# Value rows of 68 numbers per head instead of 66, and the block table's scratch inside another tile

## The chip, the cores and the metric

The kernel runs on one core of a Trainium2 chip. The time is device time in microseconds (us): 266.18 us is the median of 5 runs before the change, which lie between 265.45 and 267.64 us. Lower is better.

## The reference

Two layers follow each other. The first is a sparse attention over 4 batches of 8 heads, 768 positions and 64 numbers per head. Positions are cut into 24 blocks of 32. A query block sees its own block and its two neighbours, the first and last block, and three blocks that a table (`sampled_blocks`) draws for it. The first and last query blocks see everything.

```
scores = scale * q @ k.T ; masked entries -> -1e9
attn   = exp(scores - max) / (sum + 1e-9)
x      = attn @ v                       # 4 x 8 x 768 x 64 -> 3072 x 512
h      = x @ w_in ; r = max(h, 0) ; out = (r * r) @ w_out   # 512 -> 2048 -> 512
```

## The kernel before, in words

The order of all instructions is written out ahead of time. A planner in the kernel (`run_schedule`) holds a list of tasks with an estimated cost, a due key and the engines that may take it, and emits them one by one; after that each engine runs its own fixed list and only waits for semaphores. The estimates are constants in the file, so a change of a tile's width does not enter them.

**Batches 0 and 1 (dense with a mask).** For each pair of heads, TensorE multiplies keys by queries into PSUM (L500, and L504 for the mask rows of the first query columns), ScalarE takes the exponential into the tile `pT` (L511), VectorE multiplies by the 0/1 mask `MK` (L518), and TensorE multiplies `pT` by the values (L540). The value tile `VN` (two buffers, L370) holds, in each of 128 partitions, 6 chunks of positions x 8 heads x `VS` bf16 numbers. `VS` is 66 (L57): 64 numbers of the value, then ones. A matmul of L540 reads the first 65 (`VW`) of a head's row, so that its 65th output column is the sum of the weights, and L548 and L550 divide by it. Its output `po` is a PSUM tile whose heads stand 65 numbers apart; the pitch there is `VW`, not `VS`. The loop of L540 alternates the two heads of a pair: first head, second head, first head, and so on. Since a row has 66 numbers of 2 bytes, the first head of pair a starts 264a bytes into its chunk and the second 132 bytes after it.

**Batches 2 and 3 (sparse).** Values are cast into the same `VN` (L283 out of `cast_v`), written whole to a copy in DRAM, `vd` (L635), which has 800 rows of 8 heads x `VS` numbers, 1056 bytes; 32 rows of zeros are added to it (L631). For each of 12 query tiles, keys are gathered by VectorE and ScalarE into `KG`, and values are brought back from `vd` into a tile `VG`: the window rows and the rows of the global blocks by SP's queue (L693, L699), the rows of the drawn blocks by indirect DMAs that GpSimd (POOL) issues (L703, one for each query block, 96 rows each, by the row numbers `idx`). There are two `VG`: one lies in the raw-input tile `RAW`, the other in the mask tile `MK`; DMA rows name these. Scores are L715 and L720, exponentials L727, and values L761: four query blocks at a time in the four column groups of TensorE, weights of 128 x 32, moving rows of 65 numbers out of `VG` or `VN`, outputs again 65 apart.

**The second layer** runs between these tasks as TensorE becomes free: L810 (512 -> 2048), L819 or L821 (relu), L830 or L832 (square), L860 (2048 -> 512), then a copy and a store.

**The block table.** At the start VectorE builds the 24 x 24 table of visible blocks in a scratch tile `al` (24 x 4 x 24 fp32, L380, written by L386 to L391, reduced by L393), which sets the mask rows `bm` (L394). `KG1` (L331) is a tile of 4096 bf16 per partition that later holds one of the two `KG`; at the start its first 2304 numbers hold three helper tables, and the numbers from 2304 on serve later as scratch for the row numbers (L585, six pieces of 72 fp32).

Of the kernel before, what the change touches and what calls it, by code (L numbers as in the profile page):

```python
# [12 lines left out]
F32 = mybir.dt.float32  # L13
# [12 lines left out]
def kernel(  # L26
# [12 lines left out]
    B, H, S, D = q.shape  # L39
    block = 32  # L40
    nb = S // block
    n_rand = sampled_blocks.shape[1]
# [11 lines left out]
    TWM = 768  # L54
    NU = B * HP
    VW = D + 1
    VS = D + 2  # L57
    ND = 2
    NT = NCH
    SEQ = [NT - 1] + list(range(NT - 1))  # L60
# [5 lines left out]
    consts = ctx.enter_context(tc.tile_pool(name="consts", bufs=1))  # L66
# [264 lines left out]
    KG1 = consts.tile([P, HP * 4 * 256], BF, name="KG1")  # L331
# [36 lines left out]
    for i in range(2):  # L368
        QKB.append(consts.tile([P, HP, 2, S], BF, name=f"QK{i}"))
        VN.append(consts.tile([P, NCH, H, VS], BF, name=f"VN{i}"))  # L370
        G.memset(VN[i][:, :, :, D:VS], 1.0)
    QK = [QKB[u // HP % 2][:, u % HP] for u in range(NU)]
# [4 lines left out]
    V.tensor_copy(out=oh.rearrange("a (n p) -> a n p", p=P), in_=place.rearrange("a (p n) -> a n p", n=NCH))  # L377
    edge = consts.tile([nb, 2], F32, name="edge")
    pm = consts.tile([nb, 2, nb], F32, name="pm")
    al = consts.tile([nb, n_rand + 1, nb], F32, name="al")  # L380
    V.tensor_scalar(out=pm[:, 0, :], in0=rel, scalar1=-1.0, scalar2=None, op0=AOP.is_ge)
    V.tensor_scalar(out=edge[:, 0:1], in0=row, scalar1=0.0, scalar2=None, op0=AOP.is_equal)
    V.tensor_scalar(out=edge[:, 1:2], in0=row, scalar1=float(nb - 1), scalar2=None, op0=AOP.is_equal)
# [27 lines left out]
    KG = [x.rearrange("p (a i c) -> p a i c", a=HP, i=4) for x in KG]  # L411
    VG = [flat[1][:, 0:8 * H * VS], MK.rearrange("p n s -> p (n s)")[:, 0:8 * H * VS]]
    VG = [x.rearrange("p (i c d) -> p i c d", i=4, c=2) for x in VG]
# [163 lines left out]
    at16 = consts.tile([1, (nb - 2) * n_rand], I32, name="at16")  # L577
    vd = {b: dram.tile([S + block, H * VS], BF, name=f"vd{b}") for b in range(ND, B)}
    picked_of = sbb.rearrange("p (q r two) -> p q r two", r=n_rand, two=2)[:, 1:nb - 1, :, 0]
# [44 lines left out]
    def zero_rows(part, e):  # L624
        if part == 0:
            z = work.tile([P, 2, 512], BF, name="pT", tag="pT", bufs=PT_BUFS).rearrange("p h c -> p (h c)")
            V.memset(z[0:block, 0:H * VS], 0.0)
            stmp["z"] = z[0:block, 0:H * VS]
        else:
# [582 lines left out]
```

## Time and profile before

| what | value |
|---|---|
| median of 5 runs | 266.18 us (265.45 to 267.64) |
| the profiled execution's own time | 265.65 us |
| its span, first to last instruction | 263.9 us |
| granted TensorE clock | 1.00 |
| busy: VectorE / ScalarE / POOL | 155.4 / 199.2 / 138.2 us |
| DMA moved | 46.40 MB in 62992 packets, 176 GB/s on average |
| value rows back from `vd` by SP's queue | 12 + 8 transfers of 198 KB, 4 of 99 KB, 16 of 66 KB |
| value rows back by POOL's indirect DMAs | 44 (20 into `RAW`, 24 into `MK`), 916 to 1173 ns of POOL each |
| `vd` written | 2 transfers of 792 KB |

A row of the chain of work reads: start in the span, length, engine, tile and line, and how many instructions. PE is TensorE, DVE is VectorE, ACT is ScalarE, SP and POOL issue DMAs. A group row reads: instruction, count, shortest, median and longest duration in ns, first and last start. Durations of matmuls are from issue to a modelled end and overlap; what a matmul costs TensorE is the distance from one start to the next, or a run's length in the chain divided by its count.

### The profile page before, as it was taken

The numbers are of one execution on the slowest core, as the hardware profiler recorded it, in microseconds if no ns is written. First come the engines' busy times: TensorE is split into PE (matmuls) and PEld (weight loads), VectorE is DVE, ScalarE is ACT, GpSimd is POOL, SyncE is SP. The second block draws the span as 40 slices with busy tenths as digits, with TensorE's granted clock in tenths as the row PEclk, the third lists the DMA queues.
The fourth block names the chain that finished last, engine by engine and source line by source line (L and its number), as shares of the span: only waits on it lengthen the run. The fifth ranks groups of instructions, "written<-read, shape, count | busy, mean of one in ns | idle before, by whom it ended". The sixth has DMA issues, their size and how long they took to land.

```text
span 263.9 us, 8712 instructions
## 1 busy us (share of the span) xinstructions
PE 254.5 (96%) x3552; PEld 163.0 (62%) x3552; DVE 155.4 (59%) x452; ACT 199.2 (75%) x303; POOL 138.2 (52%) x175
## 2 busy tenths in 40 slices
PE   8999999999998899999999999999999999999994
PEld 5768866577565456656566566545665566655554
DVE  7797789999999997874554622145165535121000
ACT  3898979898989898889868898422986578945920
POOL 4391625505479700668978685540767577802610
PEclk9999999999999999999999999999999999999999
DMA  6999999979936965089966998968616645231012
GB/s 195 367 269 207 202 224 318 363 158 240 182 93 151 203 153 166 36 220 299 227 162 132 266 181 220 277 202 209 137 28 161 185 127 135 73 102 42 0 40 82
DMA packets 62992, 46.40 MB, mean 176 GB/s; under 512 B 22088, under 2 KB 57832, under 8 KB 62952
## 3 DMA queue, kind: packets, MB, share of 16 engines
q1 hardware_dynamic: 56072, 36.79, 54.8%
q0 software_dynamic: 6336, 8.66, 16.7%
q8 instruction: 28, 0.46, 0.7%
q10 hardware_dynamic: 544, 0.39, 0.5%
q14 instruction: 12, 0.10, 0.2%
HBM read 37.32 MB, written 7.98 MB: 172 GB/s over the span
## 4 chain that ended last, share of the span: by engine, by line
PE 68%; DVE 18%; DMA 5%; issue 3%; ACT 2%; SPq 2%; POOL 1%; DVEq 0%; ACTq 0%; POOLq 0%
PE py L860 25%; PE X L810 21%; DVE pT L518 10%; PE po L540 4%; PE X L761 4%; PE X L715 4%; PE X L500 3%; DMA RAW<-in_k_dram 2%; PE F L810 2%; ACT pT L511 2%; DMA MK<-vd,idx 2%; DVE xq L550 2%; PE X L860 2%; DVE qc L283 1%; SPq L300 1%
## 5 line engine op out<-in xcount | busy, mean ns | idle before, releaser
L832 POOL TENSOR_TENSOR g<-r 128x384 bf16<-128x384 f32 (+1 forms) x55 | 51.2, 936 | 80.4 <-ACT r L819 63.4
L860 PE MATMUL py<-w_out_sb,g 128*128 128x512 bf16 (+2 forms) x384 | 91.9, 368 | 0.2 <-DVE ys L283 0.2
L810 PE MATMUL X<-xT,w_in_sb 128*128 128x384 bf16 (+1 forms) x512 | 84.0, 313 | 0.0
L511 ACT ACTIVATE pT<-X 128x1024 bf16<-128x1024 f32 (+1 forms) x76 | 70.7, 979 | 9.9 <-PE X L500 6.6
L810 PEld LDWEIGHTS <-w_in_sb 128*128 128x128 bf16 x640 | 55.6, 98 | 28.0 <-issue 1.9
L819 ACT ACTIVATE r<-X 128x768 f32<-128x768 f32 (+1 forms) x61 | 46.2, 761 | 14.5 <-PE X L810 12.2
L860 PEld LDWEIGHTS <-g 128*128 128x128 bf16 x416 | 35.9, 98 | 29.5 <-issue 2.0
L518 DVE TENSOR_TENSOR pT<-pT,MK 128x1024 bf16<-128x1024 bf16 x60 | 50.3, 866 | 2.3 <-ACT pT L511 2.1
L830 ACT ACTIVATE g<-r 128x384 bf16<-128x384 f32 (+1 forms) x65 | 33.6, 540 | 1.3
L769 DVE RECIPROCAL rss<-X 128x8 f32<-128x8 f32 x12 | 2.5, 208 | 51.4 <-PE X L761 48.4
L727 ACT ACTIVATE pT<-X 128x1024 bf16<-128x1024 f32 x28 | 27.2, 1028 | 7.3 <-PE X L715 7.3
L540 PEld LDWEIGHTS <-pT 128*128 128x128 bf16 x576 | 22.5, 97 | 8.5 <-issue 4.2
L540 PE MATMUL po<-VN,pT 128*128 128x65 bf16 x576 | 24.8, 193 | 2.3 <-DVE xT L283 1.5
L703 POOL DMA_INDIRECT MK<-vd,idx x24 | 22.7, 945 | 6.8 <-issue 5.8
L500 PE MATMUL X<-QK 64*128 64x256 bf16 (+1 forms) x336 | 25.4, 257 | 0.0
L281 ACT COPY ys<-py 128x512 f32<-128x512 f32 (+1 forms) x17 | 9.9, 581 | 17.9 <-PE py L860 17.9
L703 POOL DMA_INDIRECT RAW<-vd,idx x20 | 19.1, 953 | 5.8 <-issue 4.6
L283 POOL CAST VN<-RAW 128x768 bf16<-128x768 f32 x15 | 14.8, 988 | 11.8 <-DMA RAW<-in_v_dram 11.6
L500 PEld LDWEIGHTS <-QK 64*128 64x128 bf16 x336 | 13.6, 94 | 9.9 <-issue 6.3
L283 DVE CAST qc<-RAW 128x768 bf16<-128x768 f32 (+3 forms) x22 | 14.0, 656 | 2.4 <-DMA RAW<-in_q_dram 1.3
L283 POOL CAST qc<-RAW 128x768 bf16<-128x768 f32 (+1 forms) x13 | 13.4, 1041 | 1.6 <-DMA RAW<-in_q_dram 0.8
L761 PEld LDWEIGHTS <-pT 128*32 128x32 bf16 x896 | 9.2, 95 | 5.6 <-issue 5.5
(109 smaller groups left out, 255.7 us busy)
## 6 DMA issues: line engine op xcount, KB each, us to landing
RAW<-in_v_dram SPq DMA_DIRECT2D x16, 384.0 KB, 7.4
RAW<-in_k_dram SPq DMA_DIRECT2D x15, 384.0 KB, 5.6
out_dram<-ys SPq DMA_DIRECT2D x21, 256.0 KB, 3.1
RAW<-in_q_dram SPq DMA_DIRECT2D x12, 384.0 KB, 4.0
MK<-vd SPq DMA_DIRECT2D x12, 198.0 KB, 3.8
w_in_sb<-in_moe_w_in_dram POOLq DMA_DIRECT2D x4, 512.0 KB
w_out_sb<-in_moe_w_out_dram POOLq DMA_DIRECT2D x4, 512.0 KB, 16.7
vd<-VN SPq DMA_DIRECT2D x2, 792.0 KB
```

The lines of the kernel that those rows point to most:

```text
L283: (V if e == "DVE" else G).tensor_copy(out=out, in_=in_)
L500: nc.tensor.matmul(ps[:, h, j * w:(j + 1) * w], QK[i][hs, 1, ksl], QK[i][hs, 0, qsl], start=j == 0, stop=not add, skip_group_check=True)
L511: A.activation(out=pT[:, :, 0:n], in_=stile.pop(a)[:, :, 0:n], func=AF.Exp, scale=scale)
L518: V.tensor_tensor(out=pT, in0=pT, in1=m[:, None].broadcast_to([P, 2, len(cs), w]), op=AOP.mult)
L540: nc.tensor.matmul(po[:, qc, h, :], pT[:, h, j * w + qc * P:j * w + (qc + 1) * P], VT[i][:, n, h, 0:VW], start=(n == 0 and qc == 0 and h = ...
L703: G.indirect_dma_start(out=VG[x][0:96, i, 1, :], out_offset=None, in_=vd[b][:, :], in_offset=bass.IndirectOffsetOnAxis(ap=idx[:, n:n + 1], ...
L727: A.activation(out=pT, in_=stile.pop((b, t, s_)), func=AF.Exp, scale=scale)
L810: nc.tensor.matmul(htile[T, f][:, i], w_in_sb[:, kc, (f + i) * P:(f + i + 1) * P], xT[b][:, kc, c0:c0 + w], start=(kc == 0), stop=(kc == K ...
L819: A.activation(out=to, in_=src, func=AF.Relu)
L830: A.activation(out=g, in_=r, func=AF.Square)
L832: (G if e == "POOL" else V).tensor_mul(out=g, in0=r, in1=r)
L860: nc.tensor.matmul(ytile[T, i], gtile[T, f][:, ts * P:(ts + 1) * P], w_out_sb[:, f, cs[0]:cs[1]], start=(f == 0), stop=(f == NF - 1))
```

## The change

The row of a head becomes 68 numbers (136 bytes): in `VN`, in the copies `vd` (rows of 1088 bytes), in the zero rows and in both `VG`. 4 ones follow each value instead of 2. Matmuls still read 65 numbers of a row, and PSUM keeps its pitch of 65. The two `VN` take 192 bytes more per partition each, 384 together, and `al`, which took 384 bytes, is no longer a tile of its own: it lies in the last 192 bf16 of `KG1`, behind the helper tables and behind the later scratch.

```diff
-    VS = D + 2
+    VS = D + 4
...
-    al = consts.tile([nb, n_rand + 1, nb], F32, name="al")
+    al = KG1[0:nb, KG1.shape[1] - 2 * (n_rand + 1) * nb:].bitcast(F32).rearrange("q (r j) -> q r j", j=nb)
```

On each engine the changed program has the same instructions in the same order and waits for the same engines; what differs is the extent of the ones' memsets (L371: 128 x 96 numbers before, 128 x 192 after), of the zero rows (L627, L631), of every DMA that writes or reads `vd` (rows of 528 numbers before, 544 after), and the addresses inside `VN`, `VG` and `vd`.

## The prediction

> **What bounds the kernel now.** I read first the page's busy row and chain of work, to see which engine ends last.
>
> ```profile
> PE 254.5 (96%) x3552; PEld 163.0 (62%) x3552; DVE 155.4 (59%) x452; ACT 199.2 (75%) x303; POOL 138.2 (52%) x175
> ...
> PE 68%; DVE 18%; DMA 5%; issue 3%; ACT 2%; SPq 2%; POOL 1%; DVEq 0%; ACTq 0%; POOLq 0%
> ```
>
> TensorE (PE) is busy 96% of the span, and 68% of the chain is its own work. Next the table of busy time by stretch (start:end, length, then busy us and count for PE, weight loads, VectorE, ScalarE, POOL; clock, DMA share, GB/s), to see whether that holds in the stages that read value rows.
>
> ```profile
> 20.00:60.00 40.00, 39.16 (x610) 28.67 (x607) 35.34 (x82) 35.35 (x49) 14.39 (x18) 1.00 1.06 242
> 60.00:95.00 35.00, 32.71 (x395) 21.50 (x392) 33.58 (x59) 31.44 (x42) 21.62 (x19) 1.00 0.81 174
> 95.00:110.00 15.00, 14.92 (x207) 9.57 (x202) 11.96 (x27) 13.19 (x18) 2.21 (x3) 1.00 0.39 115
> ...
> 130.00:180.00 50.00, 49.94 (x832) 29.66 (x831) 18.82 (x76) 34.08 (x58) 32.24 (x38) 1.00 0.90 207
> 180.00:240.00 60.00, 59.74 (x923) 35.98 (x922) 25.07 (x118) 41.19 (x67) 33.80 (x44) 1.00 0.47 120
> ```
>
> From 95 us on PE leaves almost nothing free; from 20 to 95 us it shares the path with VectorE's mask multiplications. So a ns saved or added on a matmul with value rows counts almost in full late and in part early. Third, the chain in order of time, for what one such matmul costs (start, length, what).
>
> ```profile
> 98.74 0.74 PE po L540 x24
> ...
> 139.51 0.93 PE X L715 x32
> ...
> 148.07 0.62 PE X L761 x63
> ...
> 213.30 0.92 POOL MK L703
> 214.22 0.30 issue
> 214.53 4.53 DMA MK<-vd,idx
> 219.05 0.04 issue
> 219.10 0.64 PE X L761 x56
> ```
>
> L540 costs 0.74/24 = 30.8 ns for 65 columns, L715 0.93/32 = 29.1 ns for 64, with the same 128 x 128 weight loads. The last lines show the one place where value rows from DRAM set the path: a gather lands 4.53 us after its issue and the matmuls of L761 wait for it.
>
> **The value matmuls of the dense half, L540.** Inside its runs the starts do not stand 30.8 ns apart but alternate: the 288 steps from a first head to its second have a median of 29 ns, the 246 from a second head to the next first one a median of 33. L715, with a new weight load for each matmul too, goes on at 29. So the second head of a pair costs 4 ns more. Two things set it apart: its moving row starts 132 bytes after the first head's, 4 past a multiple of 8, where first heads start at 264a bytes (0 or 8 past a multiple of 16); and its output starts 65 x 4 = 260 bytes after, also 4 past a multiple of 8. The change mends the first alone: heads start at 136h bytes, again 0 or 8 past a multiple of 16, where the first heads already run at 29 ns. If the moving row is the cause, 288 x 4 ns = 1.15 us of PE time go. How much lies on the path: the least is the chain's share of L540, 4% of 263.9 = 10.3 us of 576 x 31 ns = 17.9 us, 58%, so 0.66 us; the most is all of it, 1.15 us, if PE's order passes every ns on. I take the middle, -0.9 us. If the output is the cause, it is 0. A loss here I exclude: no head comes to an offset at which one runs today at over 29 ns.
>
> The Trainium skill bears on both. "PSUM — Partial Sum Buffer", section "Specifications (TRN2)", gives PSUM lines of 8 bytes and says that output patterns that aren't contiguous slow matmuls: that speaks against this change, as the second head's output still starts inside such a line, and by it the 4 ns would stay. "TensorE: Matmul & The Clock Gate", section "Back-to-back issue gap", gives N/2.4 + 2.5 ns, an estimate of 29.6 ns for 65 columns: by it L540 has 1.4 ns too much on average and 0.8 us in all to win. No row of before decides between the two.
>
> **The value matmuls of the sparse half, L761.** 0.62 us for 64, four column groups at once: 16 groups at some 30 ns after a start of two slower ones. In the tiles with no wait inside, at most three steps per tile are 4 to 6 ns over the 29 of the rest. At most 12 x 3 x 5 ns = 0.18 us can go, at least 0; they don't alternate with the heads as in L540. I take -0.05.
>
> **More bytes from and to `vd`.** SP's returns are 20 x 198 + 4 x 99 + 16 x 66 = 5412 KB, the gathers 44 x 96 x 1056 bytes = 4.46 MB, the writes 2 x 792 KB: some 11.6 of 46.4 MB, and 2/66 = 3.0% of them, 0.35 MB, is added. The packets' own time in the trace is 386 us (1056 bytes), 73 (2112 bytes) and 287 (gathers), 746 us over 16 engines: 46.6 us, of which 3% is 1.4 us. That is the upper end, if each transfer were waited for. The nearest row, the waits of PE from 132 to 240 us, has one such wait, 0.3 us:
>
> ```profile
> PE X L761 <- DMA MK<-vd,idx: 0.3, 1, 0.3
> ```
>
> There 3% of 4.53 us is 0.14 us. The other tiles hide it: for instance the gathers issued at 168.0 to 171.7 us serve matmuls at 179.1. Two are tight: those issued up to 143.0 us (matmuls at 148.0) and up to 206.0 us (209.8), at some 4.5 us to landing. Cover gone, each costs its own 0.14. A gain from better starts of rows in DRAM I take as 0: in a stretch with no other transfer, 135.6 to 138.4 us, 384 packets of 1056 bytes, of even rows and of odd ones, have a median of 47 ns and a 90th percentile of 49. I take +0.15; ends 0 and +1.4. POOL's issue (920 ns) goes by rows, which stay 96, and SP's (300 to 440 ns) by transfers.
>
> **Memsets, casts, `al`.** These rows are the tile's own view:
>
> ```profile
> L283 POOL CAST VN<-RAW x15: 823/870/1424, 10.0 to 173.6; 128x768 bf16<-128x768 f32 x15
> L371 POOL MEMSET VN<- x2: 172/174/175, 3.0 to 3.1; 128x96 bf16 x2
> ```
>
> A memset of 1024 numbers takes 947 ns (the query tile's, L677), so 96 numbers more cost at most 90 ns each, 0.18 us; POOL idles 0.79 us behind them until the first queries land at 4.0 us, so 0 on the path (without that cover, 0.18). The casts write rows 136 instead of 132 bytes apart; POOL's cast into a gapless tile takes 817 to 830 ns undisturbed, and into `VN` 823, so the spacing shows no price to win back or to lose: 0. VectorE's one cast into `VN` (1118 ns) overlaps a cast of POOL's and tells nothing. `al` keeps its five instructions, engines and waits; L386 to L393 read and write the same extents in the same order, and its new place is free until a `KG` tile is filled from 120 us on: 0. The zero rows' memset grows from 264 to 272 words: under 0.01 us.
>
> **Sum.** -0.9 - 0.05 + 0.15 = -0.8 us. Against the profiled execution's 265.65 us (span 263.9 and 1.75 around it) that is 264.85. This execution lies 0.53 below the median of the five, so on the median: 266.18 - 0.8 = 265.4 us. Differences under 0.5% (1.33 us) are about what a measurement of this kernel can't tell from no change; here that is below 264.85 or above 267.51.
>
> **Rivals.**
> 1. *The change does nothing that counts.* The output's place in PSUM, or an alternation of PE's own, makes the 4 ns. For it: L761 reads second heads at the same odd offset, and its steps do not alternate. Against it: L761 has four matmuls under way, which can hide 4 ns. Time: 266.18 + 0.15 = 266.3 us. Chance 0.25.
> 2. *Gathers land later, and PE waits (slower).* One mechanism: how a gather's rows are packed. The records of the software queue show 704 packets of 4224 bytes (four rows) and 704 of 2112 (two), so each of 16 engines moves its six rows of a gather in two packets, of median 271 and 86 ns. If four rows of 1088 bytes (4352) no longer go as one packet, each gather needs a third, at 86 to 271 ns, in the place of L703 -> L761. It decides where a tile has no slack left. For it: three of 12 tiles stand at or near zero slack. Against it: 4224 shows no bound between 4224 and 4352, and the other tiles have about 1 to 4 us. Price at 0.27 us: three tiles 0.8 us; over 0.5% needs five tiles, 1.35 us, so 266.18 + 0.15 + 1.35 = 267.7 us. Chance 0.2.
> 3. *All of it counts.* Inside the forecast: 1.15 + 0.18 with no DMA price, 264.85 us.
>
> **How the numbers follow.** Forecast (the second heads' 4 ns go) 0.55, rival 1 0.25, rival 2 0.2. The forecast spans 264.85 to 265.7 by its terms, and a median of few runs moves by some 0.5 us (the five span 2.2), so half of its chance, 0.28, I put beyond 0.5%. Faster 0.28, same 0.27 + 0.25 = 0.52, slower 0.2. Range 264.3 to 267.4: below, the lowest term less half a us; above, rival 1 and most of rival 2 with the DMA bound of 1.4 us.
>
> **What would show it.** Right: runs of L540 x24 fall from 0.74 to 0.70 us and steps stand even at 29 to 30 ns. Wrong by rival 1: still 0.74. By rival 2: packets other than 4352 and 2176 bytes in the software queue, and more than one wait of L761 for DMA. The first cast on POOL after 4.0 us starts no later; L761 stays at 0.62.

## The result, and the profile after

The time does not change: the median is 266.03 us (265.05 to 267.54, 42 runs) against 265.63 us of the kernel before (79 runs on the same chips), ratio 1.0009 with a 95% interval of 0.9998 to 1.002. In us that is +0.24, between -0.05 and +0.53. The 265.4 us of the prediction stood on a median of 266.18 from five runs; with 79 runs the kernel before lies 0.55 us lower, so the forecast of -0.8 us would have been 264.8. The profiled execution after took 266.77 us, span 265.0. In one group of runs (rows72_off8, rows68_cols64, al_only, before_again) the mean granted clock was 0.95 to 0.96 and every kernel, before too, took some 303 us, so times of that group are compared within it alone, and steps are read from the dense half, where the clock was 1.00.

The page's busy row and chain of the changed kernel:

```profile
PE 253.9 (96%) x3552; PEld 162.4 (61%) x3552; DVE 155.0 (58%) x452; ACT 198.8 (75%) x303; POOL 138.2 (52%) x175
...
PE 64%; DVE 18%; DMA 5%; ACT 4%; issue 4%; POOL 3%; SPq 0%; POOLq 0%; DVEq 0%; ACTq 0%
```

TensorE is as busy as before (0.6 us less of 254, with the same 3552 matmuls recorded). The table by stretch says the same stage by stage, in the columns of the prediction's:

```profile
20.00:60.00 40.00, 38.77 (x610) 28.40 (x607) 35.35 (x81) 34.95 (x49) 13.61 (x18) 1.00 1.07 243
60.00:95.00 35.00, 32.96 (x394) 21.73 (x394) 33.59 (x59) 31.70 (x42) 22.03 (x20) 1.00 0.75 174
95.00:110.00 15.00, 14.92 (x208) 9.65 (x204) 11.97 (x26) 13.19 (x18) 2.07 (x3) 1.00 0.41 116
...
130.00:180.00 50.00, 49.95 (x832) 29.58 (x830) 18.31 (x77) 34.12 (x58) 32.74 (x38) 1.00 1.00 209
180.00:240.00 60.00, 58.98 (x919) 35.56 (x917) 25.47 (x118) 40.62 (x66) 33.83 (x44) 1.00 0.49 124
```

In the last stretch PE is busy 0.8 us less, and its waits below are 1.0 us instead of 0.3. The chain in order of time, at the places that the prediction showed:

```profile
98.89 0.74 PE po L540 x24
...
139.66 0.93 PE X L715 x32
...
206.20 4.65 DMA RAW<-vd,idx
210.89 0.64 PE X L761 x55
...
214.35 0.92 POOL MK L703
215.57 4.69 DMA MK<-vd,idx
220.31 0.64 PE X L761 x58
```

A run of 24 value matmuls takes 0.74 us as before, and the start times in the trace still alternate: the median is 29 ns from a first head to its second and 33 from a second to the next first. Now two gathers, not one, set the path. PE's waits from 132 to 240 us:

```profile
PE X L761 <- DMA RAW<-vd,idx: 0.6, 1, 0.6
PE X L761 <- DMA MK<-vd,idx: 0.4, 1, 0.4
```

Whether these come from the wider rows is the second question of the experiments; the first is what the 4 ns come from.

### The profile page after: what moved, and what is told of

Read it like the earlier page. It is cut to its first block, busy times and chain, and to the rows that moved or that the text cites. A ratio compares the mean times of both kernels' runs of the same rounds, so it can differ in the third digit from the quotient of the medians.

```text
span 265.0 us, 8712 instructions
## 1 busy us (share of the span) xinstructions
PE 253.9 (96%) x3552; PEld 162.4 (61%) x3552; DVE 155.0 (58%) x452; ACT 198.8 (75%) x303; POOL 138.2 (52%) x175
## 4 chain that ended last, share of the span: by engine, by line
PE 64%; DVE 18%; DMA 5%; ACT 4%; issue 4%; POOL 3%; SPq 0%; POOLq 0%; DVEq 0%; ACTq 0%
PE py L860 21%; PE X L810 21%; DVE pT L518 10%; PE X L500 4%; PE po L540 4%; PE X L761 3%; PE X L715 3%; PE F L810 2%; POOL MK L703 2%; DMA RAW<-in_q_dram 2%; DMA MK<-vd,idx 2%; DMA RAW<-vd,idx 2%; DVE xq L550 2%; PE X L860 2%; DVE qc L283 2%
## 5 line engine op out<-in xcount | busy, mean ns | idle before, releaser
L860 PEld LDWEIGHTS <-g 128*128 128x128 bf16 x416 | 35.9, 98 | 29.6 <-issue 2.0
L540 PEld LDWEIGHTS <-pT 128*128 128x128 bf16 x576 | 22.4, 97 | 7.6 <-issue 3.3
L540 PE MATMUL po<-VN,pT 128*128 128x65 bf16 x576 | 24.7, 193 | 1.6 <-DVE xT L283 1.0
L283 DVE CAST qc<-RAW 128x768 bf16<-128x768 f32 (+3 forms) x22 | 13.4, 629 | 2.7 <-DMA RAW<-in_q_dram 1.8
L761 PEld LDWEIGHTS <-pT 128*32 128x32 bf16 x896 | 9.3, 94 | 6.5 <-issue 6.4
```

The costliest lines, as they stand in the source:

```text
L283: (V if e == "DVE" else G).tensor_copy(out=out, in_=in_)
L540: nc.tensor.matmul(po[:, qc, h, :], pT[:, h, j * w + qc * P:j * w + (qc + 1) * P], VT[i][:, n, h, 0:VW], start=(n == 0 and qc == 0 and h = ...
L860: nc.tensor.matmul(ytile[T, i], gtile[T, f][:, ts * P:(ts + 1) * P], w_out_sb[:, f, cs[0]:cs[1]], start=(f == 0), stop=(f == NF - 1))
```

## The experiments

**What makes the second head 4 ns longer.** The change had put every moving row on 8 bytes and nothing moved. Left were the output's place in PSUM, the odd 65 columns, both together with the row's place, or something of TensorE's own.

psum66, on the kernel before:

```diff
-        return t[:, 0:w // P * 2 * VW].rearrange("p (c h d) -> p c h d", h=2, d=VW)
+        return t[:, 0:w // P * 2 * PW].rearrange("p (c h d) -> p c h d", h=2, d=PW)   # PW = D + 2
-                    nc.tensor.matmul(po[:, qc, h, :], pT[...], VT[i][:, n, h, 0:VW],
+                    nc.tensor.matmul(po[:, qc, h, 0:VW], pT[...], VT[i][:, n, h, 0:VW],
```

and the same in L742 and L761 (`...` stands for what is left out of a line; the comment is added here).

> The kernel before with one thing changed: value outputs stand 66 instead of 65 numbers apart in PSUM, so every head starts on a multiple of 8 bytes; rows of 66 in SBUF and matmuls of 65 columns stay. Theory A, the output's place makes the 4 ns of the second head: steps of L540 become 29 to 30 ns for both heads, a run of 24 falls from 0.74 to 0.70 us, time 0.66 to 1.15 us less. Theory B, the odd number of 65 columns makes it: steps stay at 29 and 33, time the same. Theory C, an alternation of TensorE's own with 65 columns whatever their place: as B here, and not changed by 66 columns either.

Measured: medians 29 and 33, mean step 31.1 ns, ratio to before 1.0004 (0.9985 to 1.0023). The output's place is not the cause.

cols66: as psum66, with `0:PW` for `0:VW` in output and moving row.

> As psum66, and each value matmul reads and writes 66 columns (the 66th repeats the sum of the weights). Theory A: as psum66, steps of both heads even, at about 30 ns (one column more is 0.4 ns). Theory B: here the alternation goes, steps even at about 30 ns, while psum66 keeps it. Theory C: 29 and 33 stay. Time by A or B 0.4 to 0.9 us less than before (L540 gains up to 1.15 us, 576 columns more cost 0.24 us), by C 0.1 to 0.3 us more.

Measured: 29 and 33, mean 31.2 ns, ratio 1.0006 (0.9989 to 1.0024). An even number of columns does not help, so theory B fell, and of the three only theory C had its signs right.

rows68_psum66: the changed kernel with the edits of psum66.

> The changed kernel (rows of 68) with outputs 66 apart in PSUM: both places even. If only the two together matter (a matmul runs at 29 ns when moving row and output both start on 8 bytes), steps are even here and in no other kernel, time 0.66 to 1.15 us less than the changed kernel. By theory A: as psum66, plus what the wider rows cost (0 to 0.3 us). By B and C: steps of 29 and 33.

Measured: 29 and 33, mean 31.1 ns, ratio to before 1.0011 (0.9993 to 1.0029). Row and output both on 8 bytes do not help. Of the chain in order of time, the same run of 24 in each kernel; psum66, cols66, rows68_psum66:

```profile
98.87 0.75 PE po L541 x24
```

```profile
97.80 0.74 PE po L541 x24
```

```profile
97.76 0.74 PE po L541 x24
```

The first surprise came from rows72, made for the other question (its edit is below): 30.6 ns, both heads with a median of 29, and a longer step of 35 every fourth or fifth matmul instead of 33 every second. With this theory C fell as well: at the same 65 columns another layout changes the alternation. The rows of rows72 start on multiples of 16 bytes, so two variants moved them.

rows72_off8:

```diff
-        copy(e, VT[u][:, :, :, 0:D], raw[u][2].rearrange("p t n d -> p n t d"))
+        copy(e, VT[u][:, :, :, O:O + D], raw[u][2].rearrange("p t n d -> p n t d"))   # O = 4
-                    ... VT[i][:, n, h, 0:VW],
+                    ... VT[i][:, n, h, O:O + VW],
```

and the same in L756 and L759. `VS` and `sbb` are as in rows72, and further memsets write the ones in front of the values.

> Rows of 72 numbers as in rows72, but the values stand 4 numbers into their rows and the ones behind them, so that every moving row starts 8 bytes past a multiple of 16, where in rows72 every one starts on a multiple of 16 (mean step of L540 there 30.6 ns, no alternation by head). Theory D, the place of a row's start in a 16-byte line sets the step: no alternation, but a higher mean, 31 to 33 ns. Theory E, that neighbouring matmuls start at different places in such a line makes the alternation (66: 4 apart, 68: 8 apart, 72: none): as rows72, mean 30.6 with a longer step every fourth or fifth. Time within 0.3 us of rows72 by both.

Measured: mean 30.2 ns, no alternation by head, so theory D fell; ratio to the kernel before in the same group 1.0026 (0.998 to 1.0072).

rows72_second8: as rows72_off8, with `4 * h` in the place of `O`.

> Rows of 72, first heads on a multiple of 16 bytes, second heads moved 4 numbers into their rows, 8 bytes past a multiple of 16 (the offsets of the changed kernel at the pitch of rows72); each cast into the value tile is two casts of one head. Theory E, unequal places of neighbours in a 16-byte line make the alternation: 29 and 33 are back, mean 31.1 ns. If the pitch of 144 bytes itself made rows72 even: no alternation by head, mean 30.2 to 30.6. Time within 0.5 us of rows72 by both.

Measured: mean 30.3 ns, medians 29 after a first head and 31 after a second. Neither expectation held whole. The mean is that of the other kernels of 72, but the longer steps, of 32 to 36 ns, are back behind the second heads: 120 of their 246 steps against 1 of 288 behind first heads, so that in most runs every second pair has one (29, 28, 30, 33 ns and again). In rows72 steps of 33 to 36 ns stand behind both, 64 and 52. So at this pitch the place of a row's start does bear on which head the longer step follows, as theory E has it, though not on the mean: 30.6, 30.2 and 30.3 ns in the three. (Time, one run each: 265.25 us beside 265.84 before, which shows nothing.)

What the three kernels of 72 share, and no other, is the pitch of 144 bytes and that `pT`, the weights of L540, lies 192 bytes further on. The two were not tried apart. But al_only, below, has rows of 66 and a `pT` that lies 384 bytes nearer, and it still steps 29 and 33 with a mean of 31.2: moving `pT` is not enough in itself. What a move by 192 bytes does, no run shows.

rows68_cols64, and cols64_again, the same kernel at the full clock:

```diff
-                    nc.tensor.matmul(po[:, qc, h, :], pT[...], VT[i][:, n, h, 0:VW],
+                    nc.tensor.matmul(po[:, qc, h, 0:D], pT[...], VT[i][:, n, h, 0:D],
-        V.reciprocal(out=rs, in_=po[:, :, :, D:VW])
+        V.reciprocal(out=rs, in_=po[:, :, :, 0:1])
```

and the same in the sparse half.

> The changed kernel with value matmuls of 64 columns; it leaves out the sums of the weights and divides by the first value column instead. First heads start on a multiple of 16 bytes, second heads 8 past one. Theory D or E, the place alone: steps of 29 and 33 stay. Theory F, the 65th column, 2 bytes past the eighth 16-byte line, is needed for the extra time: steps of L540 even at 29, as in L715 with its 64 columns; a run of 24 takes 0.70 instead of 0.74 us, and L761's steps of 33 to 35 go. Time by F 0.5 to 1.3 us less than the changed kernel, by D or E the same.

> rows68_cols64 once more (rows of 68, 64 columns; leaves out the sums of the weights and divides by the first value column), for its time at the full clock: L540's mean step there was 29.6 instead of 31.15 ns, 0.9 us of TensorE less over 576, and L761 gives up to 0.1 us. If 58 to 100% of it reaches the end, 0.5 to 1.0 us less than before, ratio 0.996 to 0.998; if the dense half hides it, ratio 1.000.

Measured: mean 29.6 ns in both, steps of 30 and 29. So the part of theory F on the steps held: the extra 4 ns need columns beyond the 64th. The weights are the same and lie where they did, so they alone do not make the alternation. Whether the number of columns does it or the bytes that the 65th lies on, these kernels do not tell apart. rows68_cols64 took 1.0003 (0.9961 to 1.0044) of before, cols64_again 0.9985 (0.9968 to 1.0003), 0.4 us less, where 0.5 to 1.0 was expected; both intervals hold 0. The same run of 24 in rows72, rows72_off8, rows72_second8 and cols64_again:

```profile
98.21 0.73 PE po L540 x24
```

```profile
97.74 0.72 PE po L541 x24
```

```profile
98.17 0.72 PE po L541 x24
```

```profile
98.54 0.71 PE po L540 x24
```

**What a ns of L540 is worth at the end.** dense_cols96, on the kernel before:

```diff
-                    nc.tensor.matmul(po[:, qc, h, :], pT[...], VT[i][:, n, h, 0:VW],
+                    nc.tensor.matmul(po[:, qc, h, :].rearrange("p (r d) -> p r d", r=2), pT[...], VT[i][:, n, h, None, 0:48].broadcast_to([P, 2, 48]),
```

with `po` 96 apart and the reciprocal as in rows68_cols64.

> What a ns of L540 is worth at the end: the kernel before with value matmuls of the dense half of 96 columns (the first 48 numbers of a row, read twice); it leaves out the other 16 value columns and the sums of the weights, and divides by the first column. A step should take 96/65 of the columns: some 42 to 43 ns instead of 31.15 on average, 576 x 11.5 = 6.6 us of TensorE more. If all of it lies on the path (the prediction's upper end): about 6.6 us more, ratio 1.025. If the chain's share of 58% does (its lower end): 3.8 us, ratio 1.014. If the matmuls are mostly beside VectorE's work: under 2 us, ratio under 1.008.

Measured: the steps have medians of 42 and 43 ns and a mean of 42.9 (31.15 before, counted alike), 576 x 11.8 = 6.8 us more of TensorE, and the time is 1.014 (1.0108 to 1.0172) of before, 3.7 us (2.9 to 4.6). So 55% (42 to 67) of the added time reaches the end: near the chain's share of 58%, and not the middle towards 100% that the prediction took. With 96 columns, out of the first 48 numbers of a row, nothing like 29 and 33 appears: more than 64 columns alone do not bring it. The same run of 24, and the one wait of PE for a gather from 132 to 242 us:

```profile
101.33 1.02 PE po L540 x24
```

```profile
PE X L761 <- DMA MK<-vd,idx: 0.3, 1, 0.3
```

**What the bytes cost.** rows72, on the changed kernel:

```diff
-    VS = D + 4
+    VS = D + 8
-    sbb = consts.tile([3 * block, nb * n_rand * 2], I32, name="sbb")
+    sbb = KG1[0:3 * block, 3200:3200 + 4 * nb * n_rand].bitcast(I32)
```

> Rows of 72 numbers: 9.1% more bytes from and to the DRAM copies, three times what the change adds (1.05 MB instead of 0.35); the raw block table lies inside KG1 as well, to make room. If bytes are what the change costs (the changed kernel's profile has 1.0 us of waits of L761 for gathers against 0.3): waits of L761 of 2 us or more, time 0.5 to 2 us above before. If a gather's time to landing is set by its issue and latency: landing stays at 4.4 to 4.7 us, waits between 0.3 and 1.0 us, time within 0.3 us of the changed kernel. Steps of L540 stay at 29 and 33 by every theory that is left.

Measured: ratio to before 1.0001 (0.9975 to 1.0026) with three times the added bytes. Its waits of L761, and those of psum66, whose rows have 66 numbers:

```profile
PE X L761 <- DMA RAW<-vd,idx: 0.6, 1, 0.6
PE X L761 <- DMA MK<-vd,idx: 0.5, 1, 0.5
```

```profile
PE X L762 <- DMA MK<-vd,idx: 0.5, 1, 0.5
PE X L762 <- DMA RAW<-vd,idx: 0.5, 1, 0.5
```

before_third, the kernel before once more:

> The kernel before, one profile more, for the waits of L761 for gathers at the full clock: if they differ between executions and not between widths, one or two waits of 0.3 to 0.6 us; if 0.3 us is what rows of 66 cost, one wait of 0.3 us or less.

Measured: one wait for a gather.

```profile
PE X L761 <- DMA MK<-vd,idx: 0.5, 1, 0.5
```

So rows of 66 have one or two such waits, of 0.3 to 0.5 us, and the changed kernel's two are not its own. Taken as the time that the two tiles near 210 and 219 us need beyond the 0.495 us of an undisturbed one, five profiles with rows of 66 lost 0.5, 0.6, 0.9, 0.9 and 1.4 us, three with rows of 68 lost 0.7, 1.3 and 1.5, two with rows of 72 lost 1.5 each. That leans to some tenths of a us for wider rows; so few profiles, whose values for 66 and 68 overlap, do not show it.

**`al` alone, and the measurement itself.** al_only is the changed kernel with `VS = D + 2`; before_again is the kernel before.

> The change's other part alone: the block table's scratch in KG1's tail, rows of 66 as before. Every theory: instructions L386 to L393 keep their durations (285, 59, 59, 215, 303 ns), time within 0.2 us of before; a longer opening (the first casts later by 0.1 us or more) would mean that the new place is waited for.

> The kernel before, unchanged, profiled once more. If the waits of L761 for gathers differ between executions and not between widths (psum66 with rows of 66 had two of 0.5 us, cols66 one of 0.5, rows72 0.6 and 0.5, the changed kernel 0.6 and 0.4, before 0.3): one or two waits of 0.3 to 0.6 us here too. If 0.3 is what rows of 66 cost: again a single wait of 0.3 us or less. Time the same.

Measured: L386, L391 and L393 take 285, 215 and 303 ns in al_only as before, and its ratio is 1.0033 (1.0002 to 1.0064). The unchanged kernel beside it has 1.0045 (1.0003 to 1.0087): there the same program misses 1 by more than al_only does, so al_only shows no cost, and no interval of that group is good for half a per cent. before_again's waits do not answer their question: none of its longest waits was for a gather.

## Why the prediction was right, and where it was not

The range of 264.3 to 267.4 us held, and within 0.5% was the likeliest outcome. The mechanism of the forecast was wrong; what happened is the outcome of rival 1, which had a chance of 0.25. That the number held all the same owes to how little was at stake and to a range that reached from the forecast to both rivals: as far as the mechanism goes it was luck. Of the two causes that rival 1 names, the output's place is refuted (psum66), and an alternation of PE's own does not stand in every layout (rows72).

- **"the second head of a pair costs 4 ns more"**: the step after a second head is 4 ns longer in every kernel with 65 or 66 columns and rows of 66 or 68. That the second head costs it, and not the first head that follows, is a reading of the step that no run tests.
- **"Two things set it apart"**: this is the step that failed. From two differences the prediction made the only two causes. The row's start on 8 bytes is not it (the change: 33 ns stay), the output's place is not it (psum66), and both together are not it (rows68_psum66). The runs showed a condition that was not on the list, columns beyond the 64th, and a second one that came with rows of 72. The term of -0.9 us is 0: the mean step is 31.15 ns before and 31.13 after.
- **"I take the middle, -0.9 us"**: the middle between 58 and 100% was too high as well. dense_cols96 gives 55% (42 to 67), so 4 ns less on 288 matmuls would have brought some 0.6 us, 0.24%: under what can be told here even with the mechanism right. (The 10.3 us behind the 58% are 3.9% of the span, not the rounded 4%.)
- **The PSUM rule of the Trainium skill** ("PSUM — Partial Sum Buffer", "Specifications (TRN2)") speaks of patterns that aren't contiguous. The 65 outputs of a head are contiguous in every kernel here, so the step from it to the 4 ns was the prediction's own; with outputs on 8-byte lines psum66 still alternates at a mean of 31.1 ns. The formula N/2.4 + 2.5 ns of "TensorE: Matmul & The Clock Gate", section "Back-to-back issue gap", is given there for an isolated matmul, and the section expects more than it gives at few columns where each matmul has a weight load of its own, as here. All the same the estimates from it, 42.5 ns for 96 columns and 29.2 for 64, agree with the traces: medians of 42 and 43, and means of 29.1 (L715) and 29.6 (L540 with 64 columns). For 65 its 29.6 is 1.5 under the 31.1 of this kernel.
- **Bytes, +0.15 us, ends 0 and +1.4**: the change's interval of -0.05 to +0.53 us holds the 0.15 and excludes the upper end; rows72, at -0.7 to +0.7 us, excludes three times the upper end, but not three times 0.15. The packets' own time did not grow as the bytes did: the sum over all value rows and gathers is 707 to 746 us in five full-clock profiles of rows of 66, 759 to 814 in three of 68 (3% more bytes) and 793 and 814 in two of 72. Over 16 engines the means differ by 3.0 us from 66 to 68, twice the 1.4 of the prediction, and still no run shows it at the end. A packet of 1088 bytes took a median of 48 ns in the quiet 64 packets near 56 us, against 47 for 1056 bytes.
- **L761, -0.05**: an undisturbed tile of 64 takes 492 to 495 ns in both: 0.
- **Memsets**: the two of the ones took 248 instead of 173 ns each, 0.15 us together. The first cast on POOL stands at 4.20 instead of 4.05 us, but waits 0.79 us for its queries in both profiles, and rows72, with a memset twice as wide again, starts L540 0.02 us after the kernel before: nothing on the path, as predicted. One small price was not foreseen: VectorE's L386, which runs beside these memsets, takes 285 ns with rows of 66, 299 in the changed kernel and 620 in rows72; in al_only it is 285, so it goes with the memsets and not with `al`.
- **Rival 2**: did not happen. The software queue's records hold 704 packets of 4352 and 704 of 2176 bytes, so four rows still go as one packet. Its second sign, more than one wait of L761, did appear, but appears with rows of 66 as well; it was no good sign.

Open stays what makes the steps uneven at 65 columns and why they are 0.5 to 0.9 ns shorter on average in the three kernels of 72. At 576 matmuls and 55% that is worth 0.2 to 0.3 us, so none of them can be shown to be faster.

## What to carry to other kernels

A pattern in start times that follows a layout is not yet an effect of that layout: list what else alternates or could matter (count of columns, output, weights) and bound the gain before spending memory on it. Here the bound was there: 4 ns x 288 matmuls x the chain's share of the line is 0.66 us, a quarter of a per cent. The share of a line in the chain of work was a good exchange rate from its own time to the end in this one trial (58% read, 55% measured, 42 to 67), better than the busy share of its engine (96%). It holds for a small change alone: in dense_cols96 the chain has gone over to L540, whose share there is 8.2% of 267.2 us, 21.9 of its 24.7 us.

## What the runs showed that was not expected

In before_again the unchanged kernel took 38 us more, all of it after 130 us: the dense half kept its steps, while some runs of 64 matmuls of L761 took up to 4.5 us instead of 0.5, with PE waiting for nothing that the profile shows. PE's longest waits from 132 to 290 us:

```profile
PE X L761 <- issue: 14.0, 27, 1.2
PE X L715 <- issue: 5.7, 1, 5.7
```

The pauses came before the lower clock. The first stretch of them and the stretch after it, in the columns of the table by stretch:

```profile
132.70:135.80 3.10, 1.45 (x58) 0.94 (x59) 0.00 (x0) 1.52 (x3) 2.43 (x3) 1.00 0.45 100
135.80:142.60 6.80, 5.29 (x113) 4.31 (x113) 2.36 (x16) 1.03 (x2) 1.75 (x2) 0.50 0.43 103
```

Five times from 133 to 269 us the granted clock falls from 1.00 to 0.50, for 3.4 or 6.8 us. Each time PE had begun to pause 2 to 4 us earlier, at a clock of 1.00; shorter pauses, as at 233 us, were followed by no fall. So the lower clock did not start the pauses. What did, no run shows.
